# Channel attention and a gated convolution on one core: which queue issues the output stores

## The chip, the core and the metric

The kernel runs on one core of a Trainium2 chip. The core has a matrix engine (TensorE, PE in the profile), a vector engine (VectorE, DVE), a scalar engine (ScalarE, ACT), a general engine (GpSimd, POOL) and SyncE (SP), which computes nothing. Each engine works through its own instruction list in order. A DMA is an instruction in the list of the engine that issues it: when its turn comes it waits there for its semaphores, and whatever stands behind it in the same list waits with it. The transfer itself then runs on 16 DMA engines that all queues share. The metric is the device time of one execution in microseconds (us), as the median of three runs.

## The reference, cut to what matters

There are four batches of 6336 rows with 256 channels.

```python
def _attn_ref(q, k, v, tau):
    qn = q / (np.linalg.norm(q, axis=1, keepdims=True) + 1e-06)
    kn = k / (np.linalg.norm(k, axis=1, keepdims=True) + 1e-06)
    s = kn.transpose(0, 2, 1) @ qn / tau          # 256 x 256 per batch
    a = softmax(s)                                # over the last axis
    return v @ a

def _moe_ref(x, w_val, conv_w, w_out):            # x is the result above
    gate = sigmoid(sum(conv_w[k] * x_shifted_by(4 - k) for k in range(5)))
    return (gate * (x @ w_val)) @ w_out
```

(The softmax, the sigmoid and the causal convolution over five rows are written out in the original.) So each batch has two stages. The first reads all of q and k and makes a 256 x 256 matrix. The second reads v, multiplies it by that matrix, gates it, and writes the output rows.

## The kernel before, in words

**Tiles.** The first stage goes over groups of up to three blocks of 128 rows (`score_group`). For a group, q and k are loaded by SyncE into one of six `raw` buffers (L90, L92), ScalarE rounds them to a high part (`hi`, L276), GpSimd makes the remainder (L277), ScalarE squares them (L295), VectorE and GpSimd add the squares up (L300), and TensorE accumulates the scores (`s_ps`, L324). The second stage goes over chunks of 508 rows, 13 to a batch and 52 in all (`all_steps`). In one step TensorE makes the input of the convolution (`x_ps`) and the value (`val_ps`, both L549), ScalarE and VectorE make the gate (L563, L567, L573), VectorE multiplies (L585), ScalarE and GpSimd split the result into two parts (`split_g`, L598 and L599), and `finish` multiplies it by `w_out` (`o_ps`, L618), has ScalarE copy it from PSUM to the tile `o_sb` (L628), and stores `o_sb` to the output (L633 and L635).

**Loads of v.** v is needed with channels on the partitions. Early steps load rows (`v_raw`, L445 to L451) and transpose them on TensorE (`t_ps`, L539, copied by ScalarE in L540). Steps 5 to 41 take half of the channels by a transposing DMA (`h_cols`, L502), spread it by four more DMAs (`h_parts`, L511) and join it on VectorE (`h_word`, L526). Steps 42 to 50 take all channels in that way (`v_cols` L463, `v_parts` L473, `v_word` L489). SyncE issues all of these loads.

**Between the batches.** When the last group of a batch is done, `softmax` works through a chain across the engines: the scores are copied from PSUM by ScalarE (`s`, L354), the sums of squares are collected on TensorE (L357, L359) and their roots taken by ScalarE (L367, L374), VectorE inverts them (L375, L376), GpSimd scales the scores (L378, L384, L385), VectorE finds the extreme of a row (`m`, L387), ScalarE takes the exponential (L390, with a load of its table ahead of it) and adds a small constant (L392), VectorE inverts the sum (L394), GpSimd scales (`a`, L400), TensorE transposes the matrix (L410) and multiplies it by `w_val` (L421). The convolution of the next batch needs that matrix. Groups of the next batch's scores are interleaved with the steps of this one. There are no more groups to interleave after those of the last batch.

**What sets the order.** The program is written as one long list: a loop over the steps calls the loads, the groups, the softmax pieces (`tick`) and the parts of a step. A planner that simulates the time of the instructions then puts each engine's list in order; `issue_after` and the helper `behind` add the constraint that an instruction stands behind a named one on its engine. So the place of a store among its engine's other instructions is the planner's choice. The planner also adds the semaphore waits. Tiles of the pool `w_p`, `o_sb` among them, have two buffers.

**The queues.** SyncE issues every load, and of the stores those of step 50 (the last but one) and one of the two of step 51, which has stores of its own (L626). ScalarE issues the stores of steps 0 to 49, two to a step: one of all whole blocks of 128 rows (L633), one of the rows left over (L635).

Of the kernel before, what the change touches and what calls it, by code (L numbers as in the profile page):

```python
# [37 lines left out]
def kernel(  # L38
# [13 lines left out]
    nc = tc.nc  # L52
# [549 lines left out]
    def finish(b, i):  # L602
        t0, w = chunks[i]
        gh, gl = gts.pop((b, i))
        nt = -(-w // P)
        offs = [min(j * P, w - P) for j in range(nt)]
        o_sb = w_p.tile([P, NT, C], F32, name="o_sb")
        for j in range(0, nt, 2):
            pair = offs[j:j + 2]
            last = (b, i) == all_steps[-1]  # L610
            o_ps = ps.tile([P, 512], F32, name="o_ps", tag="bank")
            halves = [o_ps, ps.tile([P, 512], F32, name="o_ps", tag="bank") if last and len(pair) > 1 else o_ps]
            for u, off in enumerate(pair):
                n_ = 0
                o_ps = halves[u]
                for h in range(NH):
                    for gs, ws in ((gh, wo_hi), (gh, wo_lo), (gl, wo_hi)):
                        marks["OUT"] = nc.tensor.matmul(o_ps[:, u * C:(u + 1) * C], gs[:, h, off:off + P], ws[:, h, :],  # L618
                                                         start=n_ == 0, stop=n_ == 3 * NH - 1)
                        n_ += 1  # L620
            if (b, i) == all_steps[-1]:

                for u, (copy, dma) in enumerate(((nc.scalar.copy, nc.scalar), (nc.vector.tensor_copy, nc.sync))[:len(pair)]):
                    copy(o_sb[:, j + u, :], halves[u][:, u * C:(u + 1) * C])
                    first = max((j + u) * P - pair[u], 0)
                    dma.dma_start(out=out[b, t0 + pair[u] + first:t0 + pair[u] + P], in_=o_sb[first:P, j + u, :])  # L626
                continue
            marks["ACT"] = nc.scalar.copy(o_sb[:, j:j + len(pair), :], o_ps[:, 0:len(pair) * C].rearrange("p (j c) -> p j c", c=C))  # L628
        if (b, i) == all_steps[-1]:
            return  # L630
        full = w // P
        store = nc.sync if (b, i) == all_steps[-2] else nc.scalar
        store.dma_start(out=out[b, t0:t0 + full * P].rearrange("(j p) c -> p j c", p=P), in_=o_sb[:, 0:full, :])  # L633
        if w % P:
            store.dma_start(out=out[b, t0 + full * P:t0 + w], in_=o_sb[P - w % P:P, full, :])  # L635
# [3 lines left out]
    all_steps = [(b, i) for b in range(B) for i in range(NC)]  # L639
# [150 lines left out]
    for n in range(len(all_steps)):  # L790
# [65 lines left out]
        if prev:  # L856
            with behind(*{len(all_steps) - 2: ["CONV"], len(all_steps) - 1: ["G"]}.get(n, ["CONV"] if steady else [])):
                finish(*prev)
            if steady:
                marks["O"] = marks["OUT"]  # L860
            else:
                marks.pop("O", None)
    finish(*all_steps[-1])


# [30 lines left out]
```

## Time and profile before

| | |
|---|---|
| median of three runs | 633.14 us (633.11 to 634.96) |
| the profiled execution, its own time | 635.55 us |
| its span, from the first to the last instruction | 633.7 us |
| granted TensorE clock, mean | 0.994 |
| TensorE matmul busy | 615.7 us, 97% |
| VectorE / ScalarE / GpSimd busy | 529.7 / 480.3 / 465.1 us |
| queue of SyncE's DMAs (q1) | 93.04 MB, 54.7% of the 16 engines' span |
| queue of ScalarE's DMAs (q10) | 25.32 MB, 12.8% |

Busy times do not include instructions that issue a DMA or wait for a semaphore. In rows of the timeline the columns are the start and the duration in us, the engine, the line, the operation and what it writes and reads; "x3" stands for three merged instructions, and a bracket gives the idle time of the engine ahead of the row and the instruction whose end released it. A letter q behind an engine (ACTq, SPq) marks what its queue issues: DMAs and waits. Rows of waits give the engine and line that waited, for whom, the total, how often, and the longest. Rows of stages give the length, and then the busy time and number of instructions of TensorE (PE), its weight loads (PEld), VectorE, ScalarE and GpSimd, the granted clock, the DMA share and the rate.

### The profile page before, as it was taken

Reading aid. Unit: us, or ns where it says so; the run is one execution under the profiler, and the core shown is the slowest. Engines: PE = TensorE matmul, PEld = TensorE weight load, DVE = VectorE, ACT = ScalarE, POOL = GpSimd, SP = SyncE. Lnnn points to the kernel's source line nnn. Section 1 sums busy time; section 2 is a strip of 40 time slices with the busy share of each in tenths; the row PEclk is TensorE's granted clock in tenths of the full one; section 3 lists DMA queues with packets and bytes.
Section 4 is the critical chain, followed back from the end, with each engine's and each line's share of the span. In section 5 each row is a group of like instructions: output and inputs, shape, how many; then the busy total and the mean of one; then the engine's idle time right before and its main releaser. Section 6 shows DMA issues by size and latency. Waiting matters only on the chain.

```text
span 633.7 us, 10889 instructions
## 1 busy us (share of the span) xinstructions
PE 615.7 (97%) x3845; PEld 551.8 (87%) x3845; DVE 529.7 (84%) x811; ACT 480.3 (76%) x620; POOL 465.1 (73%) x257
## 2 busy tenths in 40 slices
PE   8999999999999999999999999999996999999996
PEld 6898799999898989989988999999885897888886
DVE  4989898889889988988978999889866898877884
ACT  4787788868888787887788887877846667877754
POOL 1893689898676799989866879998855445777731
PEclk9999999999999999999999999999998899999999
DMA  8999975686736867857673779576778535692213
GB/s 256 353 358 294 326 257 173 176 230 195 181 108 177 227 206 207 238 171 218 170 211 94 232 210 233 179 231 150 177 130 186 126 103 140 141 161 67 65 53 103
DMA packets 138365, 119.06 MB, mean 188 GB/s; under 512 B 60028, under 2 KB 120390, under 8 KB 138310
## 3 DMA queue, kind: packets, MB, share of 16 engines
q1 hardware_dynamic: 112534, 93.04, 54.7%
q10 hardware_dynamic: 25776, 25.32, 12.8%
q8 instruction: 30, 0.49, 0.3%
q14 instruction: 25, 0.20, 0.1%
HBM read 65.90 MB, written 25.95 MB: 145 GB/s over the span
## 4 chain that ended last, share of the span: by engine, by line
PE 75%; DMA 11%; ACT 4%; DVE 3%; issue 3%; POOL 2%; SPq 1%; ACTq 0%; POOLq 0%
PE o_ps L618 20%; PE val_ps L549 19%; PE x_ps L549 18%; PE s_ps L324 14%; DMA raw<-in_q_dram 3%; PE t_ps L539 3%; DMA raw<-in_k_dram 3%; DMA w_raw<-in_moe_w_out_dram 1%; DMA h_cols<-in_v_dram 1%; DMA v_raw<-in_v_dram 1%; DVE gate L567 1%; PE o_ps L421 1%; DMA v_parts<-v_cols 1%; SPq L90 1%; DMA h_parts<-h_cols 1%
## 5 line engine op out<-in xcount | busy, mean ns | idle before, releaser
L567 DVE SCALAR_TENSOR_TENSOR gate<-x_ps,cw,gate 128x508 f32<-128x508 f32 (+1 forms) x416 | 276.9, 718 | 17.3 <-ACT gate L563 15.4
L277 POOL TENSOR_TENSOR hi<-raw,hi 128x1536 fp32r<-128x1536 f32 (+3 forms) x62 | 180.7, 2917 | 38.8 <-ACT hi L276 38.6
L599 POOL TENSOR_TENSOR g_lo<-gate,g_hi 128x1016 fp32r<-128x1016 f32 (+1 forms) x50 | 116.5, 2329 | 41.0 <-ACT g_hi L598 38.9
L324 PE MATMUL s_ps<-hi 128*128 128x256 f32 (+1 forms) x912 | 128.3, 286 | 0.2 <-ACT hi L276 0.2
L549 PE MATMUL x_ps<-v_hi,w 128*128 128x512 f32 (+1 forms) x376 | 125.7, 389 | 1.4 <-DVE gate L567 1.2
L300 DVE TENSOR_TENSOR acc_ps<-acc_ps,sq 128x512 f32<-128x512 f32 (+1 forms) x135 | 94.1, 697 | 35.8 <-ACT sq L295 33.8
L549 PE MATMUL val_ps<-v_hi,w 128*128 128x508 f32 (+1 forms) x376 | 120.3, 383 | 0.0
L324 PEld LDWEIGHTS s_ps<-hi 128*128 128x128 f32 (+1 forms) x912 | 117.3, 190 | 3.3 <-ACT hi L276 0.6
L618 PE MATMUL o_ps<-wo_hi,g_hi 128*128 128x256 f32 x400 | 115.2, 289 | 2.2 <-DVE gate L585 2.0
L618 PE MATMUL o_ps<-wo_lo,g_hi 128*128 128x256 f32 x400 | 112.9, 283 | 0.0
L618 PE MATMUL o_ps<-wo_hi,g_lo 128*128 128x256 f32 x400 | 112.4, 283 | 0.0
L628 ACT COPY o_sb<-o_ps 128x512 f32<-128x512 f32 x99 | 57.5, 589 | 53.7 <-PE o_ps L618 53.5
L295 ACT ACTIVATE sq<-raw 128x1536 f32<-128x1536 f32 (+2 forms) x72 | 96.0, 1342 | 0.8 <-DMA raw<-in_k_dram 0.7
L563 ACT ACTIVATE gate<-x_ps,cw 128x508 f32<-128x508 f32 (+1 forms) x104 | 68.9, 669 | 30.9 <-PE x_ps L549 27.7
L300 POOL TENSOR_TENSOR acc<-acc,sq 128x512 f32<-128x512 f32 x57 | 74.5, 1306 | 22.4 <-ACT sq L295 22.2
L585 DVE TENSOR_TENSOR gate<-val_ps,gate 128x508 f32<-128x508 f32 (+1 forms) x104 | 65.2, 659 | 29.6 <-ACT gate L573 29.1
L549 PEld LDWEIGHTS x_ps<-v_hi,w 128*128 128x128 f32 x376 | 70.0, 188 | 15.7 <-ACT v_word L489 1.6
L276 ACT CAST hi<-raw 128x1536 fp32r<-128x1536 f32 (+3 forms) x62 | 76.8, 1242 | 7.5 <-DMA raw<-in_k_dram 7.4
L549 PEld LDWEIGHTS val_ps<-v_hi,w 128*128 128x128 f32 x376 | 69.9, 189 | 12.4
L618 PEld LDWEIGHTS o_ps<-wo_hi,g_hi 128*128 128x128 f32 x400 | 76.4, 191 | 4.6 <-DVE gate L585 2.3
L618 PEld LDWEIGHTS o_ps<-wo_lo,g_hi 128*128 128x128 f32 x400 | 76.5, 191 | 1.3
L618 PEld LDWEIGHTS o_ps<-wo_hi,g_lo 128*128 128x128 f32 x400 | 76.0, 191 | 0.6
(128 smaller groups left out, 879.1 us busy)
## 6 DMA issues: line engine op xcount, KB each, us to landing
raw<-in_q_dram SPq DMA_DIRECT2D x59, 384.0 KB
raw<-in_k_dram SPq DMA_DIRECT2D x59, 384.0 KB
out_dram<-o_sb ACTq DMA_DIRECT2D x47, 384.0 KB
h_parts<-h_cols SPq DMA_DIRECT2D x124, 64.0 KB
v_raw<-in_v_dram SPq DMA_DIRECT2D x28, 256.0 KB
out_dram<-o_sb ACTq DMA_DIRECT2D x47, 124.0 KB
v_parts<-v_cols SPq DMA_DIRECT2D x36, 128.0 KB
v_raw<-in_v_dram SPq DMA_DIRECT2D x7, 512.0 KB
```

The costliest lines, as they stand in the source:

```text
L276: cast = nc.scalar.copy(hi[r, js, :, 0, :], rows_of[r, js])
L277: nc.gpsimd.tensor_tensor(hi[r, js, :, 1, :], rows_of[r, js], hi[r, js, :, 0, :].bitcast(F32), ALU.subtract)
L295: nc.scalar.activation(sq[0:np_, ja:jb], rows_of[0:np_, ja:jb], AF.Square)
L300: add = eng.tensor_tensor(st[key][0:np_], st[key][0:np_], sq[0:np_, j], ALU.add)
L324: marks["SCORES"] = nc.tensor.matmul(st["s"][:, h, :], lhs, rhs, start=False, stop=stop and h == NH - 1 and n_ == len(ops) - 1)
L549: marks["PRODUCT"] = nc.tensor.matmul(ps, wt[:, which, ws, ch, hs], vs[:, ch, lo:hi_], start=ws == 0 and ch == 0 and vs is th, stop=ws == ...
L563: marks["TAP"] = nc.scalar.activation(gate[:, h, 0:w], x_ps[:, 0:w], AF.Copy, scale=cw[:, h:h + 1])
L567: marks["GATE"] = nc.vector.scalar_tensor_tensor(gate[:, h, 0:w], x_ps[:, tap:tap + w], cw[:, tap * NH + h:tap * NH + h + 1], gate[:, h, 0 ...
L585: nc.vector.tensor_tensor(gate[:, h, 0:w], vals[h][:, 0:w], gate[:, h, 0:w], ALU.mult)
L599: marks["GL"] = nc.gpsimd.tensor_tensor(gl[:, :, 0:w], gate[:, :, 0:w], gh[:, :, 0:w].bitcast(F32), ALU.subtract)
L618: marks["OUT"] = nc.tensor.matmul(o_ps[:, u * C:(u + 1) * C], gs[:, h, off:off + P], ws[:, h, :], start=n_ == 0, stop=n_ == 3 * NH - 1)
L628: marks["ACT"] = nc.scalar.copy(o_sb[:, j:j + len(pair), :], o_ps[:, 0:len(pair) * C].rearrange("p (j c) -> p j c", c=C))
```

## The change

The store of a step's output rows is issued by SyncE in every step that reaches this line. Before, that was so for the last but one step alone. The stores of the last step (L626) are not touched: one goes by ScalarE, one by SyncE.

```diff
--- before.py
+++ after.py
@@ -629,7 +629,7 @@
         if (b, i) == all_steps[-1]:
             return
         full = w // P
-        store = nc.sync if (b, i) == all_steps[-2] else nc.scalar
+        store = nc.sync
         store.dma_start(out=out[b, t0:t0 + full * P].rearrange("(j p) c -> p j c", p=P), in_=o_sb[:, 0:full, :])
         if w % P:
             store.dma_start(out=out[b, t0 + full * P:t0 + w], in_=o_sb[P - w % P:P, full, :])
```

## The prediction

> **What bounds the kernel now.** I read the span and the busy times first, then stages of the run, then who makes TensorE wait.
>
> ```profile
> span 633.7 us, 10889 instructions
> ...
> 420.00:460.00 40.00, 40.00 (x260) 36.21 (x258) 34.16 (x49) 32.23 (x38) 35.25 (x18) 1.00 0.70 167
> 460.00:500.00 40.00, 33.93 (x193) 29.42 (x192) 26.91 (x42) 24.00 (x38) 20.93 (x16) 0.91 0.75 146
> ...
> 540.00:580.00 40.00, 40.00 (x227) 34.76 (x226) 31.62 (x49) 30.46 (x39) 29.21 (x15) 1.00 0.66 132
> ```
>
> TensorE is busy for the whole of the stages shown before and after (420 to 460, 540 to 580 us): there a microsecond saved on another engine is worth nothing. It idles 6.07 us (40.00 - 33.93) in the stage from 460 to 500. The stage with the hole is the last passage between batches: the softmax of batch 3, with no groups left to fill TensorE. Who makes it wait there, over that stage:
>
> ```profile
> PE o_ps L410 <- POOL a L400: 3.8, 2, 3.3
> PE o_ps L618 <- DVE gate L585: 2.0, 1, 2.0
> PE o_ps L618 <- ACT norms L367: 0.2, 1, 0.2
> ```
>
> Together 6.0 us. All three waits hang on ScalarE: L367 is its own, L585 needs its sigmoid (L573), `a` needs its exponential (L390).
>
> **The stores on ScalarE, in the steady state.** First their number and the length of each issue, then one ordinary step in time.
>
> ```profile
> L633 ACTq DMA_DIRECT2D out_dram<-o_sb x50: 351/383/424, 94.5 to 623.6; - x50
> L635 ACTq DMA_DIRECT2D out_dram<-o_sb x50: 276/398/618, 95.0 to 624.0; - x50
> ```
>
> ```profile
> 405.07 0.59 ACT L628 COPY o_sb<-o_ps 128x512 f32<-128x512 f32 x1 [0.83 <-PE o_ps L618]
> 405.56 1.48 ACT L276 CAST hi<-raw 128x1536 fp32r<-128x1536 f32 x1
> 405.69 0.38 ACTq L633 DMA_DIRECT2D out_dram<-o_sb  x1
> 406.12 0.40 ACTq L635 DMA_DIRECT2D out_dram<-o_sb  x1
> 406.93 1.50 ACT L295 ACTIVATE sq<-raw 128x1536 f32<-128x1536 f32 x1
> ```
>
> 50 x (0.383 + 0.398) = 39.1 us of issue leave ScalarE. But here both are issued while the 1.48 us cast runs, and the next operation starts without a gap. **I cost this at nothing**: the cast covers it, and where no cast follows (after 500 us) ScalarE waits for TensorE or VectorE behind the stores anyway. If that cover were missing, TensorE's full row of 40.00 would still hide 0.8 us in a step.
>
> **Where the stores do hold ScalarE.** In the step above the first store goes out 0.03 us after the copy ends (405.07 + 0.59 = 405.66). In the last passage the timeline shows two that stand, and they are the only ones of the run that stand a microsecond or more:
>
> ```profile
> 466.01 0.59 ACT L628 COPY o_sb<-o_ps 128x512 f32<-128x512 f32 x1 [0.84 <-PE o_ps L618]
> 471.86 0.38 ACTq L633 DMA_DIRECT2D out_dram<-o_sb  x1
> ...
> 472.80 0.59 ACT L354 COPY s<-s_ps 128x512 f32<-128x512 f32 x1 [6.20 <-PE t_ps L539]
> ...
> 480.98 1.18 ACT L628 COPY o_sb<-o_ps 128x512 f32<-128x512 f32 x2
> 486.83 0.38 ACTq L633 DMA_DIRECT2D out_dram<-o_sb  x1
> 487.24 1.28 ACT L390 ACT_TABLE_LOAD   x1 [5.09 <-DMA h_parts<-h_cols]
> 488.54 0.51 ACT L390 ACTIVATE s<-s,m 128x256 f32<-128x256 f32 x1
> ```
>
> The copies end at 466.60 and 482.16, the stores start 5.26 and 4.67 us later. The scores' copy and the exponential stand behind them. A store needs nothing but its copy as data, so this wait is one the planner added, on an earlier transfer of SyncE's queue; the chain of waits names it for the second store (the column after the start is the length):
>
> ```profile
> 483.35 0.21 DVE m L387
> 483.56 3.19 DMA h_parts<-h_cols
> ```
>
> **The change, part by part.** The scores are complete when their last matmuls end, and the rest of the softmax runs behind that:
>
> ```profile
> 465.81 2.32 PE L324 MATMUL s_ps<-hi 128*128 128x256 f32 x18
> ...
> 478.77 0.41 PE L618 MATMUL o_ps<-wo_hi,g_hi 128*128 128x256 f32 x1 [1.96 <-DVE gate L585]
> ...
> 487.51 0.40 PE L549 MATMUL x_ps<-v_hi,w 128*128 128x512 f32 x1
> 491.23 0.44 PE L410 MATMUL o_ps<-ident,a 128*128 128x128 f32 x2 [3.32 <-POOL a L400]
> 492.13 0.44 PE L410 MATMUL o_ps<-ident,a 128*128 128x128 f32 x2 [0.46 <-POOL a L400]
> ```
>
> ```profile
> 490.25 1.82 POOL L400 TENSOR_SCALAR a<-s,rz 128x256 f32<-128x256 f32 x2 [4.59 <-DVE rz L394]
> ```
>
> First wait gone: the scores are there at 465.81 + 2.32 = 468.13, so their copy starts there and not at 472.80, and roots, sigmoid, scaling and `m` come 4.67 us sooner. `m`, which starts at 483.35, starts at 478.7. The sigmoid is no longer late, so the 1.96 and 0.21 us on TensorE go. Second wait gone: the two copies of `o_sb` now follow TensorE's second block of o_ps, which without its wait starts at 478.77 - 1.96 = 476.8 and takes 12 x 0.12 (18 matmuls of the same shape end 2.32 us after the first one's start) = 1.4 us; with the copy at 0.59 ScalarE is free at 478.8, the table load of 1.28 us ends at 480.1, and the exponential starts there and not at 488.54: 8.4 us sooner. `a` then ends at 492.07 - 8.4 = 483.7. TensorE's x_ps ends at 487.91 now; without the 2.17 us of stalls and about 1.1 us of slow clock before it, at 484.6. So `a` is ready just before TensorE asks for it, and 3.32 + 0.46 go too. The margin is a microsecond; behind it `a` would be late next.
>
> Idle time saved: 0.21 + 1.96 + 3.32 + 0.46 = 5.95 us. TensorE also runs slower after each hole:
>
> ```profile
> 478.00:492.00 14.00, 9.47 (x38) 7.33 (x38) 8.15 (x13) 8.84 (x15) 8.81 (x9) 0.88 0.89 193
> 492.00:500.00 8.00, 7.87 (x45) 7.29 (x46) 7.65 (x13) 5.86 (x11) 3.76 (x3) 0.79 0.44 93
> ```
>
> That is 9.47 x 0.12 + 7.87 x 0.21 = 1.14 + 1.65 = 2.79 us. The granted clock is 1.00 in the stages shown without a hole and lower only behind the holes, so most of it should come back; I count three quarters, 2.1, since some short gap may stay. The bounds are 5.95 and 8.74; I take 8.0 in all.
>
> **What SyncE takes over.** Each store costs about 0.8 us of its queue and, being in order, holds the loads behind it until ScalarE's copy is done. Whether a load can be late is a matter of its lead:
>
> ```profile
> 404.40 0.43 SPq L90 DMA_DIRECT2D raw<-in_k_dram  x1
> 408.48 1.11 SPq L511 DMA_DIRECT2D h_parts<-h_cols  x2
> ...
> 415.79 0.42 SPq L90 DMA_DIRECT2D raw<-in_k_dram  x1
> ```
>
> ```profile
> 456.15 1.47 ACT L276 CAST hi<-raw 128x1536 fp32r<-128x1536 f32 x1
> ```
>
> The store at 405.69 falls into SyncE's gap from 404.83 to 408.48. The last load of k goes out at 415.79 and is used at 456.15: 40 us of lead. The shortest lead I find is that of the last `h_parts`:
>
> ```profile
> 512.29 2.40 SPq L511 DMA_DIRECT2D h_parts<-h_cols  x4
> 525.82 1.32 DVE L526 TENSOR_REDUCE h_word<-h_parts 128x1024 uint16<-128x1024 uint16 x1
> ```
>
> 11.1 us from the end of the issue. In the passage the two waits move onto SyncE, and with two stores (5.26 + 4.67 + 2 x 0.78 = 11.5 us) they could delay its loads; against the shortest lead less the 3.19 us that a transfer of `h_parts` took above (11.1 - 3.2 = 7.9 us) that is a loss of at most 3.6 us. I take 0, the other end: the wait is for a transfer of SyncE's own, which has to land anyway before its later loads are of use, and the leads of q and k are far longer. `o_sb` has two buffers, so a store has two steps to land. At the end nothing changes: the stores of the last two steps keep their queues.
>
> **The sum** against the profiled execution's own time (635.55, of which 1.85 lie outside the span): span 633.7 - 8.0 = 625.7, own time 627.5. That execution stands 2.4 us above the median of 633.14; against the median the forecast is 633.14 - 8.0 = **625.1 us**.
>
> **The rivals.** *No change* (633.1). The 39.1 us hide already, and the two waits could come back as others: the planner, which simulates times anew, may put something else ahead of the exponential. For it: `a` comes only a microsecond before TensorE asks. Against it: both waits are of a kind that only a DMA on ScalarE can have. The Trainium skill, "DMA: Bandwidth & Descriptors", section "Issuing engines are not separate DMA queues", says that the choice of the issuing engine is worth only the sequencer's time to issue, usually little; by it alone the result is this rival. The two rows of 5.26 and 4.67 us speak against it: it leaves the issuing engine's waits out.
>
> *Half of it.* Only one wait goes, the other is replaced. With the first alone 0.21 + 1.96 + 1.14 = 3.3, so 629.8; with the second alone 3.78 + 1.65 = 5.4, so 627.7. About 629.
>
> *Slower: SyncE's queue stalls.* The planner puts a store ahead of `h_parts` or `v_cols`, and SyncE stands at it for the copy while loads wait behind it. Place: the steps after 500 us, lead 11.1 us. It decides once SyncE stands longer than the 7.9 us worked out above. A step lasts (623.6 - 94.5) / 49 = 10.8 us in the mean, by the first and last of the 50 stores. A store one step too early, with its own issue and the next one's (1.6), holds SyncE 12.4 us and makes a hole of 12.4 - 7.9 = 4.5 us: 637.6. For it: loads and stores now share one order. The Trainium skill, "Perfetto Trace Analysis", section "DMA Optimizations", advises one engine for input and another for output; nothing here shows such a loss yet. Against it: all the leads above.
>
> *The change doesn't do what it says*: ScalarE may keep other waits on DMAs. Its remaining one issues in the last step, so I count this under no change.
>
> **How the numbers follow.** Forecast 0.50, half 0.14, no change 0.20, slower 0.16. A measurement can tell about 0.3%, 1.9 us, from no change. Forecast and half are both beyond it: faster 0.64, same 0.20, slower 0.16. The likeliest case alone runs from 633.14 - 8.74 = 624.4 to 633.14 - 5.95 = 627.2; below it I add 1.6 us, about what the three runs lie apart. The range for 8 in 10 takes in half, no change and part of slower: 622.8 to 636.
>
> **What would show it.** Right: the rows of L633 stand on SPq; the copy L354 starts within 0.5 us of the scores' last matmul; the table load of L390 starts within 1 us after the copies of `o_sb`; TensorE's waits for L400 and L585 are gone and the stage of the passage has the clock near 1.00; the steady stages are unchanged. Wrong: TensorE's idle time in the passage stays above 4 us, or waits of TensorE on DMAs of `h_parts`, `v_cols` or `raw` appear elsewhere, or ScalarE's `o_sb` copies wait for a store to land.

## The result, and the profile after

The changed kernel took **624.01 us** (median; 622.98 to 624.15). The kernel before, run beside it, took 634.05 us (633.11 to 635.07). The ratio is 0.984 with a 95% interval of 0.9815 to 0.9861. The forecast was 625.1 us, faster, and that is what came.

The page of the changed kernel, and its stage 460 to 500 us, where the kernel before had its holes, that is, stretches in which TensorE stands idle (columns: length, busy time of PE, PEld, DVE, ACT, POOL, clock, DMA share, GB/s):

```profile
span 622.2 us, 10887 instructions
```

```profile
460.00:500.00 40.00, 39.84 (x248) 35.16 (x247) 34.30 (x53) 28.37 (x45) 22.07 (x18) 1.00 0.77 177
```

TensorE's busy time in this stage went from 33.93 to 39.84 us and its clock from 0.91 to 1.00. These stages end at fixed times, so I also cut the passage by its own landmarks: from the start of the sums of squares of batch 3 on TensorE (L357) to the start of the product with `w_val` (L421). First the kernel before, then the changed one:

```profile
468.00:497.70 29.70, 23.63 (x120) 19.59 (x119) 16.61 (x26) 18.91 (x29) 12.76 (x13) 0.89 0.80 160
```

```profile
466.00:486.10 20.10, 19.95 (x120) 17.02 (x118) 15.74 (x25) 18.89 (x30) 11.99 (x13) 1.00 0.80 162
```

The same 120 matmuls take 20.1 us instead of 29.8 (29.70 is the same stretch, cut 0.1 us short). Of the 9.6 us between the two rows, 5.92 are idle time that went (6.07 to 0.15), and 3.68 are the same matmuls running faster (23.63 to 19.95), since TensorE got its full clock (1.00) for all of the passage.

The timeline of the changed kernel shows why. First TensorE's last scores, then ScalarE:

```profile
463.84 2.32 PE L324 MATMUL s_ps<-hi 128*128 128x256 f32 x18
```

```profile
464.04 0.59 ACT L628 COPY o_sb<-o_ps 128x512 f32<-128x512 f32 x1 [0.83 <-PE o_ps L618]
466.20 0.58 ACT L354 COPY s<-s_ps 128x512 f32<-128x512 f32 x1 [1.57 <-PE s_ps L324]
...
475.82 0.59 ACT L628 COPY o_sb<-o_ps 128x512 f32<-128x512 f32 x1 [0.83 <-PE o_ps L618]
476.43 1.28 ACT L390 ACT_TABLE_LOAD   x1
```

The scores are complete at 463.84 + 2.32 = 466.16, and their copy starts 0.04 us later; it had started 4.67 us late. The table load of the exponential starts 0.02 us after the copy of `o_sb` ends (475.82 + 0.59 = 476.41); it had stood 5.09 us.

The waits of SyncE show where the stores stand now (this is the longest group of them):

```profile
SPq L633 <- ACT o_sb L628: 112.7, 39, 7.9
```

SyncE stands 112.7 us at stores, up to 7.9 us at one, and TensorE loses nothing by it. The profile lists five kinds of waits of TensorE over the whole run. The longest are these, and those for L400, L585 and L367 are gone:

```profile
PE x_ps L549 <- DVE gate L567: 1.2, 1, 1.2
PE x_ps L549 <- DVE w L404: 1.1, 1, 1.1
```

The span became 633.7 - 622.2 = 11.5 us shorter. The passage gives 9.7 of it. About 2.0 us lie ahead of it (its first landmark moved from 468.0 to 466.0), and 0.2 us were lost behind it. I do not count the 2.0 us to the change. They arise in the first 93 us, in which the 16 DMA engines are almost full and no store has yet been issued (the first goes out at 94.5 and 93.0 us). First before, then after:

```profile
0.00:93.00 93.00, 87.73 (x475) 75.40 (x476) 75.05 (x125) 68.93 (x85) 59.41 (x45) 1.00 0.99 309
```

```profile
0.00:93.00 93.00, 89.86 (x488) 77.98 (x489) 75.27 (x127) 69.53 (x87) 60.09 (x45) 1.00 0.98 312
```

TensorE is 2.1 us further by then. In profiles of other kernels of this study it had done 87.88, 89.64, 89.80 and 90.21 us by 93 us with nearly all stores still on ScalarE, and 88.66 us in a second profile of the changed kernel. That is scatter, and no relation to the queue of the stores shows in it.

### The profile page after: what moved, and what is told of

The parts are those of the page before. It is cut to its first block, busy times and chain, and to the rows that moved or that the text cites. A ratio compares the mean times of both kernels' runs of the same rounds, so it can differ in the third digit from the quotient of the medians.

```text
span 622.2 us, 10887 instructions
## 1 busy us (share of the span) xinstructions
PE 612.2 (98%) x3845; PEld 550.4 (88%) x3845; DVE 528.9 (85%) x811; ACT 480.2 (77%) x620; POOL 465.7 (75%) x257
## 4 chain that ended last, share of the span: by engine, by line
PE 80%; DMA 8%; ACT 5%; DVE 5%; issue 1%; SPq 1%; DVEq 0%; ACTq 0%
PE x_ps L549 20%; PE o_ps L618 20%; PE val_ps L549 20%; PE s_ps L324 16%; PE t_ps L539 3%; DMA raw<-in_k_dram 3%; DMA raw<-in_q_dram 2%; DVE gate L567 1%; DMA w_raw<-in_moe_w_out_dram 1%; DMA h_cols<-in_v_dram 1%; PE o_ps L421 1%; DMA out_dram<-o_sb 1%; SPq L90 1%; ACT L573 1%; ACT o_sb L628 1%
## 5 line engine op out<-in xcount | busy, mean ns | idle before, releaser
L567 DVE SCALAR_TENSOR_TENSOR gate<-x_ps,cw,gate 128x508 f32<-128x508 f32 (+1 forms) x416 | 277.0, 719 | 18.6 <-ACT gate L563 16.7
L618 PE MATMUL o_ps<-wo_hi,g_hi 128*128 128x256 f32 x400 | 114.3, 286 | 0.0
L618 PE MATMUL o_ps<-wo_lo,g_hi 128*128 128x256 f32 x400 | 112.2, 281 | 0.0
L618 PE MATMUL o_ps<-wo_hi,g_lo 128*128 128x256 f32 x400 | 111.7, 282 | 0.0
L585 DVE TENSOR_TENSOR gate<-val_ps,gate 128x508 f32<-128x508 f32 (+1 forms) x104 | 65.1, 658 | 26.6 <-ACT gate L573 26.6
L618 PEld LDWEIGHTS o_ps<-wo_hi,g_hi 128*128 128x128 f32 x400 | 75.5, 189 | 1.9 <-DVE gate L585 0.2
L618 PEld LDWEIGHTS o_ps<-wo_lo,g_hi 128*128 128x128 f32 x400 | 75.6, 189 | 1.3
L618 PEld LDWEIGHTS o_ps<-wo_hi,g_lo 128*128 128x128 f32 x400 | 75.2, 189 | 0.6
```

Source lines behind the costliest of these rows:

```text
L567: marks["GATE"] = nc.vector.scalar_tensor_tensor(gate[:, h, 0:w], x_ps[:, tap:tap + w], cw[:, tap * NH + h:tap * NH + h + 1], gate[:, h, 0 ...
L585: nc.vector.tensor_tensor(gate[:, h, 0:w], vals[h][:, 0:w], gate[:, h, 0:w], ALU.mult)
```

## The experiments

My theory: the whole gain comes from two stores, those of steps 32 and 33. Each stood on ScalarE until a transfer of SyncE's queue had landed, the one ahead of the scores' copy and the other ahead of the exponential. The compiled instruction list of the kernel before names these waits (the name in brackets is the semaphore; DMAHW0 to DMAHW7 are eight that DMAs of SyncE's and of ScalarE's queue share):

```
L628 COPY o_sb<-o_ps 128x512 [waits PE]
L633 DMA out_dram<-o_sb [waits DMAHW0, Activation]
L635 DMA out_dram<-o_sb [waits DMAHW1]
L354 COPY s<-s_ps [waits PE]
...
L628 COPY o_sb<-o_ps 128x512 [waits PE]
L633 DMA out_dram<-o_sb [waits DMAHW6, Activation]
L390 ACT_TABLE_LOAD
```

"Activation" is the copy of `o_sb`, the store's data. The other semaphore has nothing to do with its data: it is the one that the store itself will raise when it has landed. The store waits until the DMA that raises it last before it in the program has landed. By the counts in the list that is a load of `v_raw` (L451) for step 32, and the first of four transfers to `h_parts` for step 33. The program's order isn't that of time: SyncE issued both after the stores were ready (466.60 and 482.16 us).

```profile
469.22 0.32 SPq L451 DMA_DIRECT2D v_raw<-in_v_dram  x1
483.56 1.24 SPq L511 DMA_DIRECT2D h_parts<-h_cols  x2
```

The rivals were the issue time of 50 pairs of stores, and the queue itself.

Every experiment edits the kernel before, unless it says otherwise. All results in one table: the median and its ratio to the kernel before, run beside it, then from each profile the start of the passage (L357), its length to L421, and the rest of the span (all in us).

| kernel | median us | ratio, 95% | start | passage | rest |
|---|---|---|---|---|---|
| before (profile shown) | 633.14 | | 468.0 | 29.8 | 135.9 |
| changed | 624.01 | 0.984 (0.9815 to 0.9861) | 466.0 | 20.1 | 136.1 |
| e1: steps 32, 33 on SyncE | 625.37 | 0.986 (0.9839 to 0.9882) | 467.0 | 20.1 | 136.5 |
| e2: all but 32, 33 on SyncE | 628.95 | 0.991 (0.9885 to 0.9937) | 466.2 | 24.9 | 136.0 |
| e3: only 32 on SyncE | 633.02 | 0.999 (0.9965 to 1.0018) | 466.2 | 29.2 | 136.0 |
| e4: only 33 on SyncE | 627.99 | 0.991 (0.987 to 0.9941) | 465.7 | 24.1 | 136.1 |
| e5: both later on ScalarE | 630.38 | 0.996 (0.9937 to 0.9975) | 465.7 | 26.4 | 136.0 |
| e8: both later still on ScalarE | 629.61 | 0.996 (0.9928 to 0.9988) | 465.7 | 25.4 | 136.0 |
| e9: 32, 33 on GpSimd | 626.86 | 0.993 (0.9907 to 0.9958) | 468.0 | 20.4 | 138.6 |
| e0: changed, again | 624.25 | 0.986 (0.9823 to 0.9893) | 466.5 | 20.1 | 136.1 |
| e6: changed, stores cut in blocks | 623.22 | 0.984 (0.981 to 0.9875) | 466.0 | 20.1 | 135.1 |
| e7: changed, stores cut in half blocks | 630.50 | 0.995 (0.9923 to 0.9975) | 466.1 | 20.1 | 143.1 |

### Two stores alone, and all but these two

```diff
-        store = nc.sync if (b, i) == all_steps[-2] else nc.scalar
+        store = nc.sync if all_steps.index((b, i)) in (32, 33, 50) else nc.scalar
```

> Only the stores of steps 32 and 33 (and of step 50, as before) are issued by SyncE; the other 48 pairs stay on ScalarE. My theory: the 9.7 us come from the waits of these two stores, which stood on ScalarE ahead of the scores' copy (L354) and the exponential (L390) in the last passage. It expects nearly the whole gain: 624 to 626 us, TensorE idle under 0.5 us between L357 and L421 of batch 3, that passage about 20 us long (29.8 before, 20.1 in the changed kernel), clock 1.00 in it. Rival one, issue time: the gain comes from some 39 us of issue that left ScalarE, spread over 50 steps. It expects 2/50 of it, so 632.5 to 633.1 us, with the two waits moved to other instructions. Rival two, waits of a like kind elsewhere in the run that are too short to be seen singly: something between, 627 to 631 us.

The passage of this kernel:

```profile
467.00:487.10 20.10, 19.93 (x120) 16.99 (x118) 15.78 (x25) 18.89 (x30) 12.08 (x13) 1.00 0.79 156
```

Measured 625.37 us. With 4 of 100 stores moved the passage is as long as in the changed kernel, and the median was in the range of my theory. The issue time of the other 48 pairs is out as the cause.

The reverse:

```diff
+        store = nc.sync if all_steps.index((b, i)) in set(range(51)) - {32, 33} else nc.scalar
```

> The reverse of the first: every store is issued by SyncE but those of steps 32 and 33, which stay on ScalarE. My theory: both waits are back ahead of L354 and L390, and nearly the whole gain is gone: 631 to 634 us, the passage 28 to 30 us long, TensorE idle about 6 us in it for POOL a L400 and DVE gate L585. It expects to keep at most the 1.5 us by which the changed kernel issued its first store sooner (93.0 us after 94.5), if these belong to the change. Rival one, issue time: 48/50 of the gain stays, 624 to 625 us. Rival two: if the two stores wait for a transfer that is on its way in any case, but now end their wait sooner since the neighbouring stores are on the other queue, 626 to 630 us with stands under 3 us each.

ScalarE in that kernel:

```profile
464.22 0.59 ACT L628 COPY o_sb<-o_ps 128x512 f32<-128x512 f32 x1 [0.84 <-PE o_ps L618]
467.30 0.43 ACTq L633 DMA_DIRECT2D out_dram<-o_sb  x1
468.23 0.71 ACTq L635 DMA_DIRECT2D out_dram<-o_sb  x1
468.98 0.59 ACT L354 COPY s<-s_ps 128x512 f32<-128x512 f32 x1 [4.18 <-PE val_ps L549]
...
477.16 1.08 ACT L628 COPY o_sb<-o_ps 128x512 f32<-128x512 f32 x2
480.95 0.40 ACTq L633 DMA_DIRECT2D out_dram<-o_sb  x1
481.39 1.28 ACT L390 ACT_TABLE_LOAD   x1 [3.15 <-DMA h_parts<-h_cols]
```

Measured 628.95 us: about half of the gain stays. My theory had said 631 to 634, and the second rival, 626 to 630 with stands under 3 us, was right. The two stores stand again, but for 467.30 - 464.81 = 2.5 us and 480.95 - 478.24 = 2.7 us instead of 5.3 and 4.7. So the length of such a wait is not a property of the store: it is how late the transfer on that semaphore is. It changes when the other stores go elsewhere; by this kernel's instruction list the store of step 32 waits for a different load of `v_raw` (L449). The two waits, 5.2 us together, lengthen the passage by 4.8 us (24.9 against 20.1).

### One of the two alone

```diff
+        store = nc.sync if all_steps.index((b, i)) in (32, 50) else nc.scalar
```

> Only the store of step 32 (the one that stood 5.26 us ahead of the scores' copy) moves to SyncE. By the prediction's working for the first wait alone (0.21 + 1.96 us of idle time and 1.14 us of slow clock) 3.3 us go: 629.5 to 630.5 us, with L354 starting within 0.5 us of the scores' last matmul, the wait for DVE gate L585 gone, and the wait for POOL a L400 still there. Rival: the two stands are one chain, the second store then waits as long as it needs for the transfer of h_parts and takes the whole gain back: 632.5 to 633.5 us. Rival: the first wait alone sets the end of the softmax: 624 to 626 us.

ScalarE in that kernel, and a row of its chain of waits:

```profile
476.04 0.59 ACT L628 COPY o_sb<-o_ps 128x512 f32<-128x512 f32 x1 [0.83 <-PE o_ps L618]
484.80 0.38 ACTq L633 DMA_DIRECT2D out_dram<-o_sb  x1
485.22 1.28 ACT L390 ACT_TABLE_LOAD   x1 [8.59 <-DMA h_parts<-h_cols]
```

```profile
480.73 4.00 DMA h_parts<-h_cols
```

Measured 633.02 us: nothing gained, where the prediction's working gave 629.8; the first rival, one chain, was right. The scores' copy is on time, everything up to the copies of `o_sb` comes sooner, and the store of step 33 then stands 484.80 - 476.63 = 8.2 us instead of 4.7. It leaves 18.6 us after the start of the passage (484.80 - 466.22), in the kernel before 18.9 us (486.83 - 467.97). When it leaves is set by the landing of SyncE's transfer (480.73 + 4.00), and ScalarE, ready 8.2 us sooner, gains nothing.

```diff
+        store = nc.sync if all_steps.index((b, i)) in (33, 50) else nc.scalar
```

> Only the store of step 33 (the one that stood 4.67 us ahead of the exponential's table load) moves to SyncE. By the prediction's working for the second wait alone (3.78 us of idle time and 1.65 us of slow clock) 5.4 us go: 627 to 628.5 us, with the wait of TensorE for POOL a L400 gone or under 0.5 us and that for DVE gate L585 (2.0 us) still there. Rival: with the first store still standing, the scores and so m come 4.67 us late, and the exponential waits for m instead of for the store: a is late by about as much as before, 631 to 633 us. If the two parts add up, the gains of this kernel and of the one with step 32 alone together make that of the one with both.

Waits of TensorE in that kernel:

```profile
PE x_ps L549 <- DVE gate L567: 2.8, 2, 1.7
PE o_ps L618 <- DVE gate L585: 1.9, 1, 1.9
```

Measured 627.99 us; the working gave 627.7. The wait for `a` is gone, that for the gate L585 stays, and one for the gate L567 of 1.7 us has come into the passage. The two parts do not add up: the passage is 0.6 us shorter without the first wait, 5.7 without the second, and 9.7 without both. The first is worth 4.0 us (24.1 - 20.1), but only once the second is gone.

### Both stores on ScalarE, placed later

```diff
+            small_done = nc.scalar.activation(norms, norms, AF.Identity, bias=small)
+            release(b, 32, small_done)
...
+        release(b, 33, at_copy)
```

`release` puts the store of that step right behind the named instruction, in batch 3 alone.

> No store changes its queue: all 50 pairs stay on ScalarE, but that of step 32 is placed behind the square root's addition (L374 of the kernel before) and that of step 33 behind the copy of at (L414), so that neither the scores' copy nor the exponential stands behind them. My theory: what counts is what stands behind a waiting store in its engine's list, not the queue that issues it. It expects most of the gain: 624 to 627 us, the passage from L357 to L421 of batch 3 at 20 to 22 us (29.8 before, 20.1 in the changed kernel); some of it may be lost where the sigmoid behind L374 now waits for the first store. Rival, the queue itself: stores and loads on two queues disturb each other in this passage, and moving a store in ScalarE's list alone helps little, 631 to 633 us. Rival, the wait only moves: the store of step 32 holds the sigmoid, TensorE waits for DVE gate L585 as before, and half is gained, 627 to 630 us.

Waits of TensorE (L595 is the kernel before's L585, its lines being shifted):

```profile
PE o_ps L628 <- DVE gate L595: 3.2, 1, 3.2
```

Measured 630.38 us, just above what the last rival gave: the exponential no longer waits for a store (of TensorE's waits for `a` 0.2 us are left), but the first store of step 32 stands 3.0 us ahead of the sigmoid (468.76 to 471.81), its second until 473.88, and TensorE waits 3.2 us for the gate that needs the sigmoid. So I moved that store behind the last of ScalarE's part of the softmax:

```diff
-            release(b, 32, small_done)
...
+        release(b, 32, nc.scalar.activation(z, z, AF.Identity, bias=tiny))
```

> As in the kernel with both stores later on ScalarE (630.38 us), all 50 pairs stay on ScalarE, and that of step 33 stays behind the copy of at (L414); but that of step 32 now goes behind the constant added to the sum (L392), the last of ScalarE's part of the softmax, instead of ahead of the sigmoid. There the 3.2 us for which TensorE waited for DVE gate L585 came from the sigmoid behind the waiting store. Theory (only what stands behind a waiting store counts): this wait goes, the passage is 20 to 21.5 us long, the median 624 to 626.5 us, with no store on another queue than before. Rival (two queues at once disturb each other, or the store of step 33 is itself too much): 628 to 633 us, with the passage over 23 us.

ScalarE in that kernel, and its chain (L400, L644 and L582 are L392, L633 and L573 of the kernel before):

```profile
478.50 0.30 ACT L400 ACTIVATE z<-z,tiny 128x2 f32<-128x2 f32 x1
482.15 0.39 ACTq L644 DMA_DIRECT2D out_dram<-o_sb  x1
482.59 0.66 ACTq L646 DMA_DIRECT2D out_dram<-o_sb  x1
483.27 1.28 ACT L582 ACT_TABLE_LOAD   x1 [4.47 <-DMA h_parts<-h_cols]
```

```profile
479.21 2.92 DMA h_parts<-h_cols
482.13 0.02 issue
482.15 0.39 ACTq L644
```

Measured 629.61 us; the rival was right and my theory's 624 to 626.5 missed. Placed 10 us later, the store of step 32 waits for a transfer that is also 10 us later: in the one kernel it left at 471.81, in this one at 482.15, straight behind a transfer of `h_parts` that the chain starts at 479.21. By the two instruction lists these are different semaphores and different transfers. It then holds the next sigmoid, and TensorE waits 4.3 us for the gate. The wait moved along with the store. For the store of step 33 the place did help: behind the copy of `at` it shows no stand in either kernel. So the theory that only what stands behind a store counts falls in that form: which transfer it waits for depends on its place too.

### The two stores on GpSimd's queue

There the instruction list gives the stores a wait for their data alone:

```
L599 TENSOR_TENSOR g_lo<-gate,g_hi [waits Activation]
L633 DMA out_dram<-o_sb [waits Activation]
L635 DMA out_dram<-o_sb
L378 TENSOR_SCALAR nk<-norms,rtau [waits DVE]
```

```diff
+        store = nc.gpsimd if all_steps.index((b, i)) in (32, 33) else nc.sync if (b, i) == all_steps[-2] else nc.scalar
```

> Only the stores of steps 32 and 33 move, and not to SyncE but to GpSimd's queue, where the instruction list gives them a wait for ScalarE's copy alone and none for a transfer. They stand there ahead of the scaling of the scores (L378) and of a (L400). Theory: the loss of the kernel before is the wait for an earlier transfer of SyncE's queue, wherever the store is placed on ScalarE; without that wait a store costs its issue only, even ahead of the softmax. It expects most of the gain: 624 to 627 us, the passage 20 to 22 us long, stores on GpSimd's queue within 1 us of what they wait for. Rival, the place in the list: a store ahead of the softmax's instructions holds them on any compute engine; GpSimd then stands some microseconds ahead of L378 or L400, 628 to 633 us. Rival, the queue of SyncE: only there is a store free of cost, 630 us or more.

GpSimd in that kernel:

```profile
465.66 2.42 POOL L599 TENSOR_TENSOR g_lo<-gate,g_hi 128x1016 fp32r<-128x1016 f32 x1
468.02 1.01 POOL L633 DMA_DIRECT2D out_dram<-o_sb  x1
469.03 0.58 POOL L635 DMA_DIRECT2D out_dram<-o_sb  x1
471.29 0.26 POOL L378 TENSOR_SCALAR nk<-norms,rtau 128x2 f32<-128x2 f32 x1 [1.67 <-DVE norms L375]
```

The store goes out as soon as the row ahead of it is done, and GpSimd then waits 1.67 us for VectorE anyway. (The store of step 33 and its second part hold `a` for 1.5 us there, and TensorE waits 0.7 us for it.) The passage is 20.4 us long, with neither of the two stores on SyncE and with both ahead of instructions of the softmax. So it is the wait for the foreign transfer that cost, neither the place nor the queue as such. The median, 626.86 us, was in the range expected. But the kernel before, run beside it, took only 630.34 us, so by the medians the gain is 3.5 us; it is the passage that speaks for the theory. The profile's start is as late as that of the kernel before, 468.0. Behind the passage 2.5 us are lost: TensorE's wait for DVE gate L567 is 2.2 us there instead of 1.2, and a stretch of 3.4 us at half the clock (0.50) follows it. Whether that belongs to the edit wasn't tried.

### How much SyncE can take

> The changed kernel itself again, beside the others of this call. The kernel with only steps 32 and 33 on SyncE took 625.37 us, 1.4 us more than the changed kernel's 624.01 in another call; their passages are equally long (20.1 us). Theory: the other 48 pairs of stores change nothing, and 1.4 us is a difference of calls: 624 to 626 us here. Rival: moving them is worth about 1 us of its own: 623.5 to 624.3 us again.

Measured 624.25 us, which lies in both ranges. The ratio is 0.986, like that of the kernel that moves two steps only (0.986). No gain of the other 48 pairs can be told from nothing: in the profiles 1.0 of the 1.4 us between these two kernels lies ahead of the passage, in its start.

In the changed kernel, each L633 store cut into one for each block of 128 rows:

```diff
+        for j in range(full):
+            store.dma_start(out=out[b, t0 + j * P:t0 + (j + 1) * P], in_=o_sb[:, j, :])
```

> The changed kernel with each L633 store cut into one DMA for each block of 128 rows: the same bytes, but two to three more issues of about 0.4 us in each step on SyncE, some 39 us over the run. The prediction costed SyncE's new work at nothing, since its loads have 11.1 us of lead or more. That theory expects no change: 623.5 to 625 us. Rival: SyncE's list is near its bound and its issue time is now part of the path: some of the 39 us comes through, 630 us or more, with waits of TensorE for DMAs of raw or for h_word that were not there.

Measured 623.22 us. 147 issues of 0.413 us (the median) instead of 51 of 0.395 are 40.6 us more for SyncE, and nothing is lost. Its standing at the stores shrinks from 112.7 to 92.9 us. The interval of its ratio overlaps that of the changed kernel, so it isn't shown to be the better one.

Then two for each block:

```diff
+        for j in range(full):
+            for x in range(2):
+                r = t0 + j * P + x * (P // 2)
+                store.dma_start(out=out[b, r:r + P // 2], in_=o_sb[x * (P // 2):(x + 1) * (P // 2), j, :])
```

> As the one before, but each block of 128 rows is stored by two DMAs of 64 rows: five to six issues instead of one in each step, at about 0.4 us each some 100 us more on SyncE in the run (about 2 us in a step of 10.8 us). SyncE stood 112.7 us in all at stores in the changed kernel, so the theory that this standing is slack expects at most a few us of loss: 624 to 627 us. Rival: the slack is used up in the last passage and the steps behind it, where loads of v are closest to their use: 628 to 640 us, with idle time of TensorE there.

The waits in which that kernel differs, and its chain (L636 is the store):

```profile
SPq L636 <- ACT o_sb L628: 30.0, 14, 4.6
...
PE val_ps L549 <- DVE v_lo L541: 4.1, 1, 4.1
```

```profile
516.10 0.60 SPq L636
517.80 0.59 SPq L511
518.44 2.09 DMA h_parts<-h_cols
521.01 1.29 DVE h_word L526
522.30 0.57 DVE v_lo L541
```

Measured 630.50 us; the rival was right. 294 issues of 0.594 us are 174.6 us, 154.5 more than in the changed kernel (I had expected 100). The standing shrinks to 30.0 us, and behind the passage a store's six issues (the last at 516.10) come ahead of the last three `h_parts` of a step, so that its word is joined late and TensorE waits 4.1 us. The rest of the span grows from 136.1 to 143.1 us.

## Why the prediction was right, point by point

**What bounds the kernel, and where the gain is.** Right. The steady stages were full and stayed so (420 to 460 and 540 to 580 us are 40.00 of 40.00 after as before); what the change gave lies in the one passage with idle time.

**The stores' issue in the steady state costs nothing.** Right: moving the other 48 pairs, too, brought no gain that can be told. By issue time alone the result would have been the rival without change. The Trainium skill, "DMA: Bandwidth & Descriptors", section "Issuing engines are not separate DMA queues", prices the choice of the issuing engine in the same way. For the 48 other pairs this case agrees with that rule; for the two it does not, since 9.7 us hung on what those instructions waited for.

**Two waits ahead of the softmax, on a transfer of SyncE's queue.** Right, and shown: by the kernel that moves these two alone (20.1 us of passage), and by the one on GpSimd's queue, where the wait is absent from the instruction list (20.4 us). Against what I had said they are not quite the only ones: the second store of a later step stands 1.4 us (558.45 to 559.89) ahead of a sigmoid. TensorE is busy for all of the 40 us around it, so it costs nothing.

**The working with both waits gone.** The idle time was right: forecast at 5.95 us, measured at 5.92. The term for the slow clock was mis-sized: forecast at 2.1 us with a bound of 2.79, while the same 120 matmuls took 3.68 us less. The kernel before shows why, with its passage divided where the clock changes:

```profile
479.00:482.40 3.40, 3.40 (x15) 3.21 (x15) 3.37 (x6) 3.15 (x5) 3.40 (x6) 0.50 1.14 196
482.50:492.60 10.10, 6.21 (x28) 4.27 (x27) 3.96 (x8) 5.28 (x9) 4.99 (x4) 1.00 0.86 201
492.70:496.00 3.30, 3.30 (x17) 3.02 (x16) 3.30 (x6) 3.30 (x7) 1.81 (x2) 0.50 0.33 79
```

The clock was at half in two stretches of about 3.4 us, and full (1.00) in the rest of the passage, its idle time included. TensorE was busy throughout both stretches, so each cost it 1.7 us, together 3.4 of the 3.68. The working multiplied the mean clock of a stage (0.88) by the busy time (9.47 us), as if the idle time had been as slow. Multiplied by the lengths of the stages, the same two rows give 14.00 x 0.12 + 8.00 x 0.21 = 3.4 us. So the bound of 2.79 was too low, and counting three quarters of it made the term smaller still. The passage gave 9.7 us, above the sum of 8.0 and the bound of 8.74.

**The margin of `a`.** The working put `a` at 483.7 and the end of x_ps at 484.6; 2.0 us sooner, as this profile lies, these are 481.7 and 482.6. In the changed kernel:

```profile
479.71 1.82 POOL L400 TENSOR_SCALAR a<-s,rz 128x256 f32<-128x256 f32 x2 [0.62 <-DVE rz L394]
```

```profile
480.91 0.39 PE L549 MATMUL x_ps<-v_hi,w 128*128 128x512 f32 x1
481.14 0.88 PE L410 MATMUL o_ps<-ident,a 128*128 128x128 f32 x4
```

`a` ends at 481.53, as worked out; x_ps ends at 481.30, 1.3 us sooner than worked out. About 0.6 us of that are the first slow stretch, which had cost 1.7 us and not 1.1; the rest I can't place. The margin I gave was not there. TensorE is held up by no more than 0.1 us all the same: the transposes of the first half need that half alone, which is ready at about 479.71 + 0.91 = 480.62 (half of the two operations' time), and the second half follows in time.

**One wait alone.** The term for the second was right in size (5.4 forecast, 5.3 measured against the kernel before run beside it), but by luck. The passage of the kernel with step 33 alone on SyncE is

```profile
465.70:489.80 24.10, 20.33 (x121) 17.01 (x119) 15.81 (x25) 18.80 (x30) 12.00 (x13) 1.00 0.89 172
```

Idle time fell from 6.07 to 3.77 us, by 2.3 and not by 3.78, since 1.7 us of a new wait came in. The busy time fell by 3.3 us and not by 1.65: both slow stretches went, although the first hole stayed (1.95 us). The term for the first wait, 3.3 us, was wrong: 0.3 us in the median. I had taken the two as a sum. The second store leaves when a transfer lands, so it swallows what the first one gives back. The rival "half" was therefore only half of a rival.

**SyncE takes the stores at no cost.** Right: it stands 112.7 us, and one of the two stores goes out 9.0 us after its copy (the copy ended at 464.63, the store was issued at 473.64) without loss. The slower rival had a place, the steps after 500 us, and a price, a hole of 4.5 us. Cutting the stores into 294 produced a hole of 4.1 us in that place, but mostly in another way: the loads came late behind six issues of a store, and not behind one that stood for a whole step. That the two prices are close is chance. The loss sets in somewhere between 40.6 and 154.5 us more of issue on SyncE. The Trainium skill, "Perfetto Trace Analysis", section "DMA Optimizations", says that it may make sense to give input and output an issuing engine each. Here, with both on one queue, the kernel is 1.6% faster, and a loss came only with the issues multiplied.

**The total.** 634.05 - 624.01 = 10.0 us by the medians, against 8.0 forecast. 1.6 us of the difference are the clock term (3.68 against 2.1), and the rest is less than what executions of the kernel before differ by. The measured 624.01 lies just below the likeliest case (624.4 to 627.2) and within the whole range.

## What to carry to other kernels

Look for instructions that stand a microsecond or more in a compute engine's list on something their data does not need, above all a DMA whose semaphore is shared with another queue. What it costs is set by the transfer that it waits for, so moving it about on the same engine may only move the wait; give it to a queue that runs no computing and has slack, or to one without the shared semaphore. When two waits lie on one chain, do not price them as a sum: ask when the second would end if the first were gone. To price a slow clock from the mean of a stage with idle time in it, multiply by the length of the stage, not by the busy time, or divide the stage where the clock changes.

## What the runs showed of the hardware that I had not expected

In the profiles of this study the granted clock stands at 1.00 or at 0.50 and nowhere between. Before the program's last microseconds it stands at 0.50 for 3.4 us at a time (once for 6.8). Matmuls of one shape (`o_ps`, L618) took 276 ns at the least and 562 ns at the most in the passage of the kernel before.

These slow stretches go with holes. Before TensorE's last matmul the twelve profiles show seven holes of 1.96 us or more (1.96, 2.20, 3.20, 3.32, 4.13, 4.28 and 7.67 us), and each has a slow stretch that starts in it or behind it. With holes of up to 1.95 us there is none. The two values beside that border come from one profile each, so it is known only roughly, and why it lies there stays open.

Executions of the kernel before scatter more than those of the changed one: 627.9 to 636.7 us against 623.0 to 625.0. Part of it goes with the clock: of the 52 executions beside the experiments the five with a mean granted clock of 0.991 took 634.7 to 636.4 us, the nine with 0.998 or more 627.9 to 632.8. That the waits on ScalarE make the scatter is not shown: with such a wait left on ScalarE the executions of a kernel lay 2.5 us (all but the two on SyncE) to 5.9 us (both later still on ScalarE) apart, without one 0.8 us (the two on SyncE) to 4.6 us (stores cut in half blocks).

A store issued by GpSimd occupies it for 0.87 to 1.01 us (L633), against 0.34 to 0.60 us on SyncE.
